# Two 256-column matmuls over one set of weights in place of a 512-column matmul

## The chip, the cores and the metric

The kernel runs on one core of one Trainium2 chip. The metric is the device time of one execution in microseconds (us). The five engines of the core that matter are TensorE (PE in the profile, with its weight loads as PEld), VectorE (DVE), ScalarE (ACT), GpSimd (POOL) and SyncE (SP), whose queue issues nearly all DMAs.

## What is computed

A layer norm of x (2048 tokens by 512) feeds two branches: attention with 32 heads of 16 over a sliding window of 256 tokens, and a SwiGLU block with 1792 hidden columns. The output is x plus the attention branch times silu of the other.

```python
xn = _layernorm(x, axis=-1)
qkv = (xn @ wqkv)                      # 512 -> 3 x 32 heads x 16
scores = einsum("bhqd,bhkd->bhqk", q, k) * 16 ** -0.5
scores = where((i - j >= 0) & (i - j < 256), scores, -1e9)
s = (softmax(scores) @ v) @ wo
g = silu((silu(xn @ w_gate) * (xn @ w_up)) @ w_down)
return x + s * g
```

## The kernel before

All tokens are worked in four chunks of 512. Float32 accuracy is reached with float32r operands: every operand is split into a high and a low part (`xh`, `xl`; `wh`, `wl`; both parts of a hidden block in `hh`), and a product is three matmuls, high by high, high by low and low by high (`PAIRS`).

The array is used in two halves. The contraction is cut into pieces of 64 rows: **half 0** holds rows 0 to 63 and **half 1** rows 64 to 127 of the same weights and inputs, and every matmul is a tile of 64 rows by 128 columns. The two halves run as two streams. Half 0 begins a unit of work, half 1 follows some microseconds later into the same PSUM bank (`LAG`), so at most moments the halves work on different units.

A unit has two items, and an item one PSUM bank of 128 by 512. There are two sorts:

- **Stationary** units (class `Stationary`, lines 509 to 534): the query/key projection (`Proj`, bank `a`) and gate and up (`GateUp`, banks `g` and `u`). The weights stand in the array and 512 tokens of `xh` or `xl` move. An item is 4 pieces of the contraction by 3 pairs, 12 matmuls of 512 columns in each half.
- **Moving** units (class `Moving`, lines 644 to 660): values (`vp`), down (`d`) and output projection (`s`). Here the activations stand in the array and 256 columns of `wh` or `wl` move, two token blocks to a bank.

Between them stand the attention matmuls, which also run on both halves: `b` (row maxima of the scores, 256 or 384 columns, line 963), `mt` (turning the maxima, line 997), `c` (scores for the softmax, line 1114, rows 0 to 48 of a half, with the negated maximum as the 49th row, which the DMA `q<-ms` writes), and `pv` (probabilities by values, line 1151). There are 32 attention units, eight to a chunk.

The order of every engine's instructions is fixed when the program is built, by a planner that keeps a clock of its own for each half. `next_mm` takes one matmul of the half whose clock is behind; `issue` advances that clock by `cols * 0.000444 + 0.004` us, 0.2313 for 512 columns and 0.1177 for 256. The other engines' instructions are put into the program as the planner's clock (`now`) reaches them, by their due times and assumed costs (`do`, `pump`), and a `pv` visit is placed where the two clocks are within 0.12 us of each other and sets both to the same time (`pv_visit`, `advance`). The planner's constants set the order alone; on the chip each instruction waits for its semaphores.

```python
steps = [(k, a, b) for k in range(KC) for a, b in PAIRS]
...
            r = min(able, key=lambda r: clock[r])
            next_mm(r)
```

Of the kernel before, what the change touches and what calls it, by code (L numbers as in the profile page):

```python
# [55 lines left out]
def tile_window_attention_swiglu_gate(  # L56
# [42 lines left out]
    clock = [0.0, 0.0]  # L99
# [124 lines left out]
    xready = {}  # L224
# [104 lines left out]
    xhigh = {}  # L329
# [40 lines left out]
    def half(r):  # L370
        return slice(R * r, R * r + R)
# [92 lines left out]
    def mm(pb, a, b, first, last):  # L464
        return nc.tensor.matmul(pb, a, b, start=first, stop=last, skip_group_check=True)  # L465
# [43 lines left out]
    class Stationary(Unit):  # L509
# [11 lines left out]
        def mms(self, i, r, pb):  # L521
            w = [t.rearrange("p (a k n) -> p a k n", a=2, k=KC) for t in self.wts(r)]
            xs = xn[self.c % 2]
            steps = [(k, a, b) for k in range(KC) for a, b in PAIRS]
            first_unit = self.c == 0 and self.n == 0 and i == 0
            if first_unit:
                steps.sort(key=lambda o: o[2])
            for k, a, b in steps:
                def go(first, last, k=k, a=a, b=b):
                    return mm(pb, w[a][half(r), i, k, :], xs[b][half(r), k, :], first, last)  # L530
                if first_unit:
                    yield 512, go, lambda k=k, b=b: (xready if b else xhigh).get((0, k))
                else:
                    yield 512, go

    class Proj(Stationary):
        def __init__(self, c, pr):
# [755 lines left out]
    front = [0.0]  # L1293
# [6 lines left out]

    def issue(r, cols):
        front[0] = max(front[0], clock[r])
        clock[r] = front[0] + cols * 0.000444 + 0.004

    def next_mm(r):
        if extra[r]:
            cols, go, then = extra[r].pop(0)
            go()
            issue(r, cols)
            if then:  # L1310
                then(clock[r] + 0.25)
            return
# [9 lines left out]
        cols, go = todo[m][:2]  # L1322
        go(r == 0 and m == 0, r == 1 and m == len(todo) - 1)
        issue(r, cols)
        if r == 0 and u.src is not None:
            work[0] += cols * MM / 512
# [62 lines left out]
    while True:  # L1389
        now[0] = max(front[0], min(clock))  # L1390
        while marks and marks[-1][0] <= work[0] / PACE - LEAD:
            _, fn, a = marks.pop()
# [8 lines left out]
        if not any(extra):  # L1401
            s = work[0] / PACE - LEAD
            for st in sorted(streams, key=lambda st: st[-1][0] if st else 1e9):
                if not st:
                    continue
                due, need, fn, a = st[-1]
# [4 lines left out]
                t = need(*a)  # L1411
# [10 lines left out]
        if able:  # L1422
            idle = 0
            r = min(able, key=lambda r: clock[r])
# [7 lines left out]
        if os.environ.get("VIRT"):  # L1432
            u, i = stream[min(pos[0], len(stream) - 1)]
# [40 lines left out]
```

## Time and profile before

| | us |
|---|---|
| median of three runs | 875.1 (871.88 to 876.57) |
| span of the profiled execution, first to last instruction | 873.5 |
| DVE busy | 520.4 (60%) |
| ACT busy | 487.7 (56%) |
| POOL busy | 621.5 (71%) |

The profiled execution's time is given only as its span of 873.5 us, which lies inside the range of the three runs, 1.6 us under their median. DMA moved 139.62 MB at a mean of 160 GB/s. The profile's page has busy time by engine, busy tenths in 40 slices, the chain of work that ended last, and groups of equal instructions (line, engine, operation, tiles written and read, partitions by elements, count; then busy time, mean ns of one and the idle time ahead of them). The timeline lists instructions in order of time: start in us, duration, engine, line, operation, tiles, count; instructions that overlap and are alike share one row with their count. A matmul's duration in these lists (392 to 395 ns for 512 columns) covers its way through the array, and the next matmul of the same half starts well before it is over; how fast a half works is read from the distance between starts.

### The profile page before, as it was taken

Reading aid. Unit: us, or ns where it says so; the run is one execution under the profiler, and the core shown is the slowest. Engines: PE = TensorE matmul, PEld = TensorE weight load, DVE = VectorE, ACT = ScalarE, POOL = GpSimd, SP = SyncE. Lnnn points to the kernel's source line nnn. Section 1 sums busy time; section 2 is a strip of 40 time slices with the busy share of each in tenths; the row PEclk is TensorE's granted clock in tenths of the full one; section 3 lists DMA queues with packets and bytes.
Section 4 is the critical chain, followed back from the end, with each engine's and each line's share of the span. In section 5 each row is a group of like instructions: output and inputs, shape, how many; then the busy total and the mean of one; then the engine's idle time right before and its main releaser. Section 6 shows DMA issues by size and latency. Waiting matters only on the chain.

```text
span 873.5 us, 30184 instructions
## 1 busy us (share of the span) xinstructions
PE 856.1 (98%) x11966; PEld 786.8 (90%) x11966; DVE 520.4 (60%) x1678; ACT 487.7 (56%) x1040; POOL 621.5 (71%) x881
## 2 busy tenths in 40 slices
PE   8999999999999999999999999999999999999997
PEld 7899989897798998989999988899899998998897
DVE  5364476656866565666578675566655775555235
ACT  3355555654665465655576546665656764566531
POOL 5556587766776778767697798677767777868761
PEclk9999999999999999999999999999999999999999
DMA  4775856576786982776687987556666779844442
GB/s 146 183 173 126 228 114 165 114 174 151 164 184 181 256 203 79 155 165 133 149 188 177 230 182 196 116 148 147 166 145 173 174 178 208 181 124 112 107 114 85
DMA packets 69488, 139.62 MB, mean 160 GB/s; under 512 B 14546, under 2 KB 23250, under 8 KB 69348
## 3 DMA queue, kind: packets, MB, share of 16 engines
q1 hardware_dynamic: 69060, 137.18, 65.3%
q8 instruction: 94, 1.54, 0.8%
q10 hardware_dynamic: 288, 0.52, 0.2%
q14 instruction: 46, 0.38, 0.2%
HBM read 107.74 MB, written 29.62 MB: 157 GB/s over the span
## 4 chain that ended last, share of the span: by engine, by line
PE 88%; DVE 4%; POOL 3%; DMA 2%; issue 1%; SPq 0%; ACT 0%; DVEq 0%; POOLq 0%; ACTq 0%
PE u L465 17%; PE d L465 17%; PE g L465 17%; PE a L465 11%; PE pv L1151 8%; PE c L1114 5%; PE s L465 5%; PE vp L465 4%; PE b L963 4%; DMA q<-ms 2%; DVE jk L971 1%; POOL wl L436 1%; DVE xt L287 1%; DMA xt<-x 1%; POOL xt L287 0%
## 5 line engine op out<-in xcount | busy, mean ns | idle before, releaser
L436 POOL TENSOR_TENSOR wl<-wr,wh 128x512 fp32r<-128x512 f32 (+3 forms) x258 | 311.7, 1228 | 92.0 <-ACT wh L433 89.8
L971 DVE CUSTOM_DVE_ANT_0 jk<-b,maskb 128x384 bf16<-128x384 f32 (+2 forms) x512 | 271.1, 529 | 119.3 <-PE b L963 53.1
L1075 ACT ACTIVATE p<-c 128x384 f32<-128x384 f32 (+1 forms) x480 | 209.7, 489 | 135.9 <-PE c L1114 107.3
L465 PE MATMUL d<-wh,hh 64*128 64x256 f32 x1792 | 258.7, 277 | 0.0
L465 PEld LDWEIGHTS d<-wh,hh 64*128 64x128 f32 x1792 | 223.5, 185 | 1.0 <-issue 0.6
L465 PE MATMUL d<-wl,hh 64*128 64x256 f32 x896 | 202.5, 276 | 0.0
L433 ACT ACTIVATE wh<-wr 128x512 fp32r<-128x512 f32 (+3 forms) x258 | 142.2, 593 | 64.4 <-PE u L465 14.1
L1088 POOL TENSOR_SCALAR_AFFINE_SELECT p<-p 128x256 f32<-128x256 f32 x256 | 107.2, 423 | 82.3 <-ACT p L1075 80.7
L465 PE MATMUL u<-xh,wh 64*128 64x512 f32 x448 | 162.1, 395 | 0.0
L465 PE MATMUL u<-xl,wh 64*128 64x512 f32 x448 | 161.3, 395 | 0.0
L465 PE MATMUL u<-xh,wl 64*128 64x512 f32 x448 | 161.3, 394 | 0.0
L465 PE MATMUL g<-xh,wh 64*128 64x512 f32 x448 | 161.2, 395 | 0.0
L465 PE MATMUL g<-xl,wh 64*128 64x512 f32 x448 | 160.6, 394 | 0.0
L465 PE MATMUL g<-xh,wl 64*128 64x512 f32 x448 | 159.4, 394 | 0.0
L465 PEld LDWEIGHTS d<-wl,hh 64*128 64x128 f32 x896 | 148.2, 185 | 0.2
L1114 PE MATMUL c<-q,k 49*128 49x384 f32 (+1 forms) x704 | 117.5, 303 | 3.5 <-DMA q<-ms 2.8
L963 PE MATMUL b<-k,q 48*128 48x384 f32 (+1 forms) x512 | 119.4, 336 | 1.2 <-DVE m L971 0.7
L1092 POOL TENSOR_SCALAR_AFFINE_SELECT p<-p 128x256 f32<-128x256 f32 x224 | 93.3, 417 | 19.0 <-ACT p L1075 18.9
L465 PE MATMUL a<-xh,wh 64*128 64x512 f32 x256 | 96.5, 394 | 0.0
L465 PE MATMUL a<-xh,wl 64*128 64x512 f32 x256 | 96.2, 392 | 0.0
L465 PE MATMUL a<-xl,wh 64*128 64x512 f32 x256 | 96.0, 393 | 0.0
L618 POOL TENSOR_TENSOR hh<-h,hh 128x512 fp32r<-128x512 f32 x56 | 72.9, 1302 | 31.7 <-ACT hh L614 31.0
(110 smaller groups left out, 2087.6 us busy)
## 6 DMA issues: line engine op xcount, KB each, us to landing
wr<-wgu SPq DMA_DIRECT2D x112, 256.0 KB
k<-qkd SPq DMA_DIRECT2D x48, 192.0 KB
wr<-wqk SPq DMA_DIRECT2D x32, 256.0 KB
qkd<-qkh SPq DMA_DIRECT2D x32, 256.0 KB
qkd<-qkl SPq DMA_DIRECT2D x32, 256.0 KB
q<-qkd SPq DMA_DIRECT2D x64, 128.0 KB
wr<-wdn SPq DMA_DIRECT2D x32, 256.0 KB
od<-ev SPq DMA_DIRECT2D x32, 256.0 KB
```

The lines of the kernel that those rows point to most:

```text
L287: (nc.gpsimd if c and i % 2 else nc.vector).tensor_scalar(xt[c, i], xt[c, i], mv[:, i, 0:1], rs[:, i : i + 1], op0=ALU.subtract, op1=ALU.mult)
L433: nc.scalar.activation(hi[0][pr, a:b], raw[pr, a:b], AF.Copy)
L436: nc.gpsimd.tensor_tensor(lo[0][pr, a:b], raw[pr, a:b], f32(hi[0][pr, a:b]), op=ALU.subtract)
L465: return nc.tensor.matmul(pb, a, b, start=first, stop=last, skip_group_check=True)
L618: nc.gpsimd.tensor_tensor(hl[:, 1, :], self.h, f32(hl[:, 0, :]), op=ALU.subtract)
L963: nc.tensor.matmul(pb[:, :w], qs[u % 3][r : r + 48, p, qb * P : (qb + 1) * P], ks[u % 3][r : r + 48, p, lo : lo + w], start=True, stop=True,)
L971: nc.vector.tensor_tensor_reduce(junk[:, :n], pb[:, :n], maskb[:, 3 * P - n :], 1.0, -3.0e38, ALU.add, ALU.max, m[:, col : col + 1],)
L1075: nc.scalar.activation(t[:, h, :], pc[:, a:b], AF.Exp, scale=DH ** -0.5)
L1088: nc.gpsimd.affine_select(s, s, [[0, 2], [1, P]], ALU.is_ge, 0.0, base=0, channel_multiplier=-1)
L1092: nc.gpsimd.affine_select(s, s, [[0, 2], [-1, P]], ALU.is_gt, 0.0, base=0, channel_multiplier=1)
L1114: nc.tensor.matmul(pc[:, at0 : at0 + w], ks[u % 3][r : r + 49, p, k0 : k0 + P], qs[u % 3][r : r + 49, p, qb * P : qb * P + w], start=(i == ...
L1151: nc.tensor.matmul(pbs[r][0][32 * j : 32 * j + 32, q0:q1], vt[half(r), (4 * c + kb) % VT, VW * (4 * g + j) : VW * (4 * g + j) + 32], t[hal ...
```

## The change

`Stationary.mms` yields two matmuls where it yielded one: the first moves tokens 0 to 255 of the chunk into columns 0 to 255 of the bank, the second tokens 256 to 511 into the other half of the bank, both with the same 64 by 128 weights. In `issue` the planner's cost of any 256-column matmul becomes 0.115 us, for the moving units and the attention matmuls of that width too; other widths keep theirs.

```diff
             for k, a, b in steps:
-                def go(first, last, k=k, a=a, b=b):
-                    return mm(pb, w[a][half(r), i, k, :], xs[b][half(r), k, :], first, last)
-                if first_unit:
-                    yield 512, go, lambda k=k, b=b: (xready if b else xhigh).get((0, k))
-                else:
-                    yield 512, go
+                for t in range(2):
+                    tok = slice(256 * t, 256 * t + 256)
+
+                    def go(first, last, k=k, a=a, b=b, tok=tok):
+                        return mm(pb[:, tok], w[a][half(r), i, k, :], xs[b][half(r), k, tok], first, last)
+                    if first_unit:
+                        yield 256, go, lambda k=k, b=b: (xready if b else xhigh).get((0, k))
+                    else:
+                        yield 256, go
...
-        clock[r] = front[0] + cols * 0.000444 + 0.004
+        clock[r] = front[0] + (0.115 if cols == 256 else cols * 0.000444 + 0.004)
```

Two places of TensorE's program show what moves. The names are the bank written, the moving tile and the weights (for `d` the weights are `hh`); the chunk's number is left out of a name, and the last number tells tiles of one name apart.

The first place is in the last chunk, with both halves on up: half 0 on `u_13`, half 1 on `u_12`. Before:

```order
L465 MATMUL u_13_16739<-xh_81,wh_16505 128x512
L465 MATMUL u_12_16665<-xh_81,wh_16505 128x512
L465 MATMUL u_13_16739<-xl_82,wh_16505 128x512
L465 MATMUL u_12_16665<-xl_82,wh_16505 128x512
L465 MATMUL u_13_16739<-xh_81,wl_16506 128x512
L465 MATMUL u_12_16665<-xh_81,wl_16506 128x512
```

And now:

```order
L465 MATMUL u_13_20153<-xh_81,wh_19809 128x256
L465 MATMUL u_12_20031<-xh_81,wh_19809 128x256
L465 MATMUL u_13_20153<-xh_81,wh_19809 128x256
L465 MATMUL u_12_20031<-xl_82,wh_19809 128x256
L465 MATMUL u_13_20153<-xl_82,wh_19809 128x256
L465 MATMUL u_12_20031<-xl_82,wh_19809 128x256
L465 MATMUL u_13_20153<-xl_82,wh_19809 128x256
L465 MATMUL u_12_20031<-xh_81,wl_19810 128x256
```

The halves still alternate one by one, but each step is half as wide and every operand pair of a half comes twice in a row.

The second place is a little later: half 1 is on gate `g_13`, half 0 on the down unit `d_2_0_0`. Before:

```order
L465 MATMUL g_13_16702<-xl_82,wh_16633 128x512
L465 MATMUL d_2_0_0_16776<-wh_16633,hh_7_16011 128x256
L465 MATMUL d_2_0_0_16776<-wh_16633,hh_8_16141 128x256
L465 MATMUL g_13_16702<-xh_81,wl_16634 128x512
L465 MATMUL d_2_0_0_16776<-wl_16634,hh_8_16141 128x256
L465 MATMUL d_2_0_0_16776<-wh_16633,hh_8_16141 128x256
```

And now:

```order
L465 MATMUL g_13_20090<-xh_81,wh_19975 128x256
L465 MATMUL d_2_0_0_20215<-wh_19975,hh_9_19779 128x256
L465 MATMUL g_13_20090<-xh_81,wh_19975 128x256
L465 MATMUL d_2_0_0_20215<-wl_19976,hh_9_19779 128x256
L465 MATMUL g_13_20090<-xl_82,wh_19975 128x256
L465 MATMUL d_2_0_0_20215<-wh_19975,hh_9_19779 128x256
```

Where one `g` stood for two `d`, the halves now take turns with equal steps.

## Prediction

> **What bounds the kernel now.** I read the page first: busy times, granted clock, and the chain that ended last.
>
> ```profile
> PE 856.1 (98%) x11966; PEld 786.8 (90%) x11966; DVE 520.4 (60%) x1678; ACT 487.7 (56%) x1040; POOL 621.5 (71%) x881
> PEclk9999999999999999999999999999999999999999
> PE 88%; DVE 4%; POOL 3%; DMA 2%; issue 1%; SPq 0%; ACT 0%; DVEq 0%; POOLq 0%; ACTq 0%
> ```
>
> TensorE has some matmul in flight for 856.1 of the 873.5 us, at an unthrottled clock, and the chain that set the end runs on it for 88%. DVE, ACT and POOL are busy for 71% at most. So the time is the sum of the steps with which TensorE's two halves take their matmuls, plus the few moments when it waits. What it waits for is in the view of waits, TensorE alone:
>
> ```profile
> PE c L1114 <- DMA q<-ms: 2.8, 3, 1.8
> PE mt L997 <- DVE m L971: 2.6, 3, 1.8
> PE xp L353 <- DVE xt L287: 2.3, 2, 1.5
> ```
>
> All of TensorE's idle time is 873.5 - 856.1 = 17.4 us, a good part of it at the start, and its longest group is 2.8 us. A change of the kernel's time by a per cent must therefore come from the steps. The groups of the page count the matmuls that the change touches:
>
> ```profile
> L465 PE MATMUL u<-xh,wh 64*128 64x512 f32 x448 | 162.1, 395 | 0.0
> ...
> L465 PE MATMUL a<-xh,wh 64*128 64x512 f32 x256 | 96.5, 394 | 0.0
> ```
>
> Up, gate and projection have three such groups each (one for each pair of high and low parts): 3 x 448 + 3 x 448 + 3 x 256 = 3456 matmuls of 512 columns, 1728 in each half. The mean of 395 ns is no step, since matmuls of one half overlap. The step is read in the timeline, where both halves are on up and nothing comes between (start, duration, then the instruction; x2 is one in each half):
>
> ```profile
> 825.05 0.40 PE L465 MATMUL u<-xh,wh 64*128 64x512 f32 x2
> 825.29 0.40 PE L465 MATMUL u<-xl,wh 64*128 64x512 f32 x2
> ...
> 826.92 0.40 PE L465 MATMUL u<-xh,wl 64*128 64x512 f32 x2
> ```
>
> From 825.05 to 826.92 each half takes eight steps: 1.87 / 8 = 0.2338 us. With the 10 ns in which starts are printed this is 233 ns, and 1728 x 0.233 = 403 us, 46% of the span. Any nanosecond on one of these steps is 1.7 us of the kernel's time.
>
> **The change, part by part.** *The step.* The change replaces 1728 steps of 233 ns in each half by 3456 of a 256-column matmul with weights from `wh` or `wl` and moving data from `xh` or `xl`. This operation isn't in the trace of before; call its step p. The sum is 1728 x (2p - 233 ns). Three other 256-column matmuls bound p. The first is down, with both halves on it:
>
> ```profile
> 217.11 0.32 PE L465 MATMUL d<-wh,hh 64*128 64x256 f32 x2
> 217.22 0.27 PE L465 MATMUL d<-wl,hh 64*128 64x256 f32 x1
> 217.27 0.34 PE L465 MATMUL d<-wh,hh 64*128 64x256 f32 x2
> 217.38 0.27 PE L465 MATMUL d<-wl,hh 64*128 64x256 f32 x1
> ...
> 218.13 0.32 PE L465 MATMUL d<-wh,hh 64*128 64x256 f32 x2
> ```
>
> Rows of two and of one alternate, so from 217.11 to 218.13 stand 18 matmuls, nine in each half: 1.02 / 9 = 113.3 ns. The second is values, in one half, while the other is on up:
>
> ```profile
> 439.00 0.39 PE L465 MATMUL u<-xh,wh 64*128 64x512 f32 x1
> 439.00 0.28 PE L465 MATMUL vp<-wh,xl 64*128 64x256 f32 x1
> 439.12 0.27 PE L465 MATMUL vp<-wh,xh 64*128 64x256 f32 x1
> 439.23 0.39 PE L465 MATMUL u<-xl,wh 64*128 64x512 f32 x1
> ...
> 440.16 0.39 PE L465 MATMUL u<-xh,wl 64*128 64x512 f32 x1
> 440.17 0.28 PE L465 MATMUL vp<-wh,xh 64*128 64x256 f32 x1
> ```
>
> `vp` starts at 439.00 and, ten steps on (two to each step of `u`), at 440.17: 117.0 ns. In the same time `u` takes five steps in 1.16 us, 232 ns. The third is the score matmul `c`, 49 rows, two of 256 columns in each half between steps of 512:
>
> ```profile
> 703.23 0.39 PE L465 MATMUL a<-xl,wh 64*128 64x512 f32 x1
> 703.46 0.41 PE L1114 MATMUL c<-q,k 49*128 49x256 f32 x4
> 703.70 0.40 PE L465 MATMUL a<-xh,wl 64*128 64x512 f32 x1
> 703.94 0.40 PE L465 MATMUL a<-xh,wh 64*128 64x512 f32 x1
> ```
>
> The half that works on `a` takes its two `c` from 703.46 to 703.70, so p = 120 ns. The three ends of the sum: with 113.3, 1728 x (226.6 - 233) = -11.1 us; with 117.0, 1728 x (234 - 233) = +1.7 us; with 120, 1728 x (240 - 233) = +12.1 us. **I take 116.5 ns**, half of what 512 columns take now, sum 0. The nearest row is `vp`: it reads the same two sets of buffers as the changed products (`x` and `w`, their roles swapped), while `d` reads the hidden blocks. In the window quoted, `vp` and the 512-column `u` beside it go at the same pace for a column: 117.0 / 256 = 0.457 ns and 232 / 512 = 0.453 ns. So the column, not the instruction, seems to set the step for these buffers, and cutting in two moves nothing.
>
> *The weight loads.* Every matmul of before has a load of its own (11966 and 11966 on the page), also `d`, whose high part stays in the array for two products in a row. So I count on 3456 more loads, over weights that are there already. What hides them is the half's own matmul:
>
> ```profile
> L465 PEld LDWEIGHTS d<-wh,hh 64*128 64x128 f32 x1792 | 223.5, 185 | 1.0 <-issue 0.6
> ```
>
> A load of this shape shows 185 ns, yet down issues one for every step of 113.3 ns in a half, so loads overlap too. Cost beyond p: none. If that cover were gone, p would grow towards the 185 ns of the load.
>
> *The planner's constant and the finer steps.* 0.115 in place of 0.1177 us brings the planned step of the moving units nearer to the traced 113 to 117. It costs no instruction; it shifts where attention matmuls, other engines' work and DMA issues fall in each engine's program. Nothing is moved by more than the drift between two clocks. Bounds from the waits: the three listed above add up to 7.7 us, so -3 to +6 us; I take 0, since the row of waits does not say to which side.
>
> *The `pv` visits.* Each sets both halves to one time, and the half that is ready first waits for the other. The planner allows a visit when its clocks are within 0.12 us; with steps of 233 ns the halves miss each other by up to 117 ns, with 116 ns by up to 58, so on average some 30 ns less. The chain of waits, in order of time, shows one visit thus, and there are 32:
>
> ```profile
> 796.02 2.38 PE pv L1151 x93
> ```
>
> 32 x 0.03 = 1.0 us, an estimate, at the least 0 and at the most twice that. I take -1.0 us.
>
> **The sum:** 0 + 0 + 0 - 1.0 = -1 us on a profiled span of 873.5 us, which gives 872.5. That execution's span is 1.6 us under the median of the runs, and I carry the difference over: 875.1 - 1.0 = **874.1 us**.
>
> **The rivals.** *The step falls to down's 113.3 ns.* For it: down has 256 columns, its own load for each, the same row count, and holds 113.3 whatever the order of its pairs; in the changed program nearly all neighbours have one width, as in that stretch of `d`. Against it: `vp` has all that too and needs 117. Fully, 874.1 - 11.1 = 863.0 us; at 115 ns, 1728 x (230 - 233) = -5.2, 868.9 us.
>
> *A fixed cost for each matmul*, the one that ends slower. Its place is the start of each of the 1728 added steps in a half; `c` shows it, with 120 ns between 512-column steps of 233 to 240. At 120 the kernel takes 874.1 + 12.1 = 886.2 us, at 118.5 it takes 1728 x 4 = 6.9 more, 881.0. It decides from p = 117.8: there the sum passes +4.4 us, half a per cent. Against it: `c` has one row more, other buffers, and weights that change with each piece; `vp` at 117.0 stays below.
> The Trainium skill, "TensorE: Matmul & The Clock Gate", section "Back-to-back issue gap", has the gap as the columns over the clock plus a fixed 2.5 ns for each matmul, so that two of 256 take 2.5 ns longer than one of 512; an estimate from that is 1728 x 2.5 ns = 4.3 us, 878.4 us. The trace differs: twice down's step is less than the 512-column step, twice `vp`'s is about equal, and only `c` goes that way.
>
> *The new order makes new waits.* The DMA `q<-ms` made TensorE wait 3 times in 32 units, 2.8 us, 0.9 us each. Six more such units would be +5.6 us, 879.7. For it: that row is the longest wait, and every transfer's place moves. Against it: TensorE is in no hurry if its steps don't shorten.
>
> *The change does nothing of its kind*, if the built program merged or dropped a load: excluded by the program, where all 3456 pairs stand.
>
> **How the numbers follow.** The same pace for a column (p between 115.5 and 117.8): 0.50, of which with the shift of waits some 0.11 fall below -0.5% and 0.08 above +0.5%. The faster step: 0.27, nearly all of it faster. The fixed cost: 0.15, nearly all slower. New waits alone: 0.08, half slower. This gives faster 0.37, same 0.37, slower 0.26; half a per cent, 4.4 us, is about what a measurement of this kernel can tell from no change. The range must reach into both rivals: down to 865 (p of 114 ns), up to 882 (p of 118.5 with 1 us of waits); left out are about a tenth on each side. The likeliest case alone is 870 to 879.
>
> **What would show it.** In the changed profile's timeline, a stretch with both halves on up: ten steps in 1.13 us say the first rival, 1.17 the forecast, 1.20 the second. The groups must list 6912 matmuls of 256 columns for `a`, `g` and `u`, and as many loads. TensorE's waits should stay near 17 us in all; if they grow by 5 or more, it is the order. The forecast is wrong if the step leaves 115.5 to 117.8, or if one half waits for the other in a way that neither shows as idle.

## The result and the profile after

The changed kernel takes 896.7 us (893.33 to 900.09, four runs) against 873.6 us for the kernel before in the same series: a ratio of 1.0257, 95% interval 1.0229 to 1.0285, so 20 to 25 us slower. The profiled execution has a span of 897.7 us and took 899.62 us. The forecast was 874.1 us, and its range ended at 882.

The page after, the lines that answer to those of before: busy times and the chain that ended last.

```profile
PE 870.8 (97%) x15422; PEld 838.3 (93%) x15422; DVE 527.5 (59%) x1678; ACT 487.5 (54%) x1040; POOL 618.3 (69%) x881
...
PE 77%; DMA 13%; DVE 4%; POOL 2%; SPq 2%; issue 2%; ACT 1%; DVEq 0%; ACTq 0%; POOLq 0%
```

Two things have changed. TensorE has 3456 more matmuls and as many more loads, as the program said, and is busy 14.7 us longer. And its idle time, in which both halves stand still, has grown from 17.4 to 897.7 - 870.8 = 26.9 us. The chain shows the same: it runs through DMAs for 13% of the span, where it was 2%.

The groups of the page (line, engine, operation, tiles; count, busy time and mean ns) count the split products, and the timeline gives their step:

```profile
L465 PE MATMUL u<-xh,wh 64*128 64x256 f32 x896 | 172.9, 280 | 0.0
```

```profile
848.45 0.27 PE L465 MATMUL u<-xh,wh 64*128 64x256 f32 x1
...
851.29 0.27 PE L465 MATMUL g<-xh,wh 64*128 64x256 f32 x1
```

One half begins an item of `u` at 848.45 and the next item, a `g`, at 851.29. An item is now 24 matmuls in each half, so the step is 2.84 / 24 = 118.3 ns, two of them 236.6 where 512 columns took 233.

The waits of TensorE (who waited for whom; total us, times, longest) show where idle time was added:

```profile
PE mt L1000 <- DVE m L974: 6.2, 4, 2.9
PE c L1117 <- DMA q<-ms: 5.4, 6, 1.7
PE d L465 <- DVE ho L462: 2.6, 1, 2.6
```

The turning of the maxima waits 6.2 us for DVE (2.6 before), the scores 5.4 us for the maxima's DMA (2.8 before), and one down unit 2.6 us for DVE's handover copy. These are the waits of one execution: in a second profile of the same kernel, the "change again" below, the turning waits 3.4 us in all, the scores 2.5, and the down unit 2.6 again.

### The profile page after: what moved, and what is told of

It is laid out like the page before. It is cut to its first block, busy times and chain, and to the rows that moved or that the text cites. A ratio compares the mean times of both kernels' runs of the same rounds, so it can differ in the third digit from the quotient of the medians.

```text
span 897.7 us, 37111 instructions
## 1 busy us (share of the span) xinstructions
PE 870.8 (97%) x15422; PEld 838.3 (93%) x15422; DVE 527.5 (59%) x1678; ACT 487.5 (54%) x1040; POOL 618.3 (69%) x881
## 4 chain that ended last, share of the span: by engine, by line
PE 77%; DMA 13%; DVE 4%; POOL 2%; SPq 2%; issue 2%; ACT 1%; DVEq 0%; ACTq 0%; POOLq 0%
PE d L465 16%; PE u L465 14%; PE g L465 13%; PE a L465 8%; PE pv L1154 6%; DMA q<-ms 5%; PE s L465 5%; PE c L1117 5%; PE b L966 4%; PE vp L465 3%; DMA r<-rd 2%; DMA den<-od 2%; SPq L95 2%; DMA k<-qkd 1%; DMA q<-qkd 1%
## 5 line engine op out<-in xcount | busy, mean ns | idle before, releaser
L1078 ACT ACTIVATE p<-c 128x384 f32<-128x384 f32 (+1 forms) x480 | 209.1, 489 | 139.6 <-PE c L1117 117.8
L465 PE MATMUL g<-xh,wh 64*128 64x256 f32 x896 | 173.4, 281 | 0.4 <-issue 0.4
L465 PE MATMUL u<-xh,wl 64*128 64x256 f32 x896 | 172.9, 280 | 0.0
L465 PE MATMUL u<-xh,wh 64*128 64x256 f32 x896 | 172.9, 280 | 0.0
L465 PE MATMUL g<-xl,wh 64*128 64x256 f32 x896 | 172.3, 281 | 0.0
L465 PE MATMUL g<-xh,wl 64*128 64x256 f32 x896 | 172.1, 280 | 0.0
L465 PE MATMUL u<-xl,wh 64*128 64x256 f32 x896 | 170.8, 280 | 0.0
L465 PEld LDWEIGHTS g<-xh,wh 64*128 64x128 f32 x896 | 134.1, 186 | 0.9 <-issue 0.7
L465 PEld LDWEIGHTS g<-xh,wl 64*128 64x128 f32 x896 | 134.4, 187 | 0.4 <-issue 0.2
L465 PEld LDWEIGHTS u<-xh,wh 64*128 64x128 f32 x896 | 133.8, 186 | 0.6 <-issue 0.4
L465 PEld LDWEIGHTS g<-xl,wh 64*128 64x128 f32 x896 | 134.2, 187 | 0.2
```

What stands on the lines that cost most here:

```text
L1078: nc.scalar.activation(t[:, h, :], pc[:, a:b], AF.Exp, scale=DH ** -0.5)
```

## The experiments

The theories. **A:** the step itself is dearer. **B:** the new order of the instructions makes the loss. **C:** the order hurts only because TensorE is slower than the planner's 0.115 us. **D:** each order draws its own waits, spread and by luck. **E:** the order's waits sit at the chunk boundaries, where DVE stands in its queue behind two late DMAs. All ratios are to the kernel before, on the same chip, with their 95% intervals.

### The split in the old order

```diff
-                    return mm(pb, w[a][half(r), i, k, :], xs[b][half(r), k, :], first, last)
+                    for t in range(2):
+                        tok = slice(256 * t, 256 * t + 256)
+                        mm(pb[:, tok], w[a][half(r), i, k, :], xs[b][half(r), k, tok], first and t == 0, last and t == 1)
```

> Both halves of each 512-column product are issued as two 256-column matmuls, but the planner counts them as one step of 512 columns, so all other instructions of every engine stand in the order of before. Theory A (the step itself is dearer: about 118.5 ns in the changed profile against half of 233, 4 to 5 ns for each of 1728 pairs in a half): 8 us over before, about 881 to 883 us. Theory B (the loss is only the new order's waits): within 2 us of before. If the split alone carries the whole loss, about 896.

1.0078 (1.0049 to 1.0106), 880.3 us: 0.0078 x 875 = 6.8 us. The step read from the trace gives (236.6 - 233) x 1728 = 6.2 us. Over some 2600 products that follow each other directly in both profiles, the pair takes 3.9 ns more on the mean than the single matmul of before, which is 6.7 us for 1728. Theory A is right about the step, and the step is under a third of the loss of the first series.

### The planner's constant alone

```diff
-        clock[r] = front[0] + cols * 0.000444 + 0.004
+        clock[r] = front[0] + (0.115 if cols == 256 else cols * 0.000444 + 0.004)
```

> Only the planner's cost of a 256-column matmul becomes 0.115 us; the products stay 512 columns wide. Theory A (the step and the order share the loss): the order moves with little change of the step, so any time over before is waits; some us up to 10. Theory B (the order of the moving units alone makes the waits): most of the 23 us, near 890 or more. If neither the constant nor its order matters: 872 to 876.

1.0033 (1.0012 to 1.0055), 2.9 us. The reordering of the moving units alone costs little.

### Other constants with the split

The changed kernel with the old formula, and with three other constants in place of 0.115:

```diff
-        clock[r] = front[0] + (0.115 if cols == 256 else cols * 0.000444 + 0.004)
+        clock[r] = front[0] + cols * 0.000444 + 0.004
```

> The products are split as in the change, with the planner's old cost (0.1177 us for 256 columns). Theory A: the plan is now close to the traced step of 118.5 ns, so the waits shrink and about 8 us of step remain: 880 to 884. Theory B with the finer steps as the cause of the waits: still 890 or more.

> The change with 0.1185 us in the planner for 256 columns, the traced step. Theory C (the gap between planned and real step makes the waits): 879 to 883, the 6.8 us of the step and no more. Theory D (each constant draws another order, and the waits are luck): anything from 879 to 896, in no order with the constant.

> The change with 0.113 us, further below the real step. Theory C: more waits than with 0.115, over 897. Theory D: anything from 879 to 900.

> The change with 0.1165 us, between the change's 0.115 and the old 0.1177. Theory C: between their times, 886 to 896. Theory D: anything from 879 to 896.

| planned step, us | ratio to before |
|---|---|
| 0.113 | 1.0129 (1.0087 to 1.0171) |
| 0.115 (the change) | 1.0257 (1.0229 to 1.0285) |
| 0.1165 | 1.0241 (1.0186 to 1.0295) |
| 0.1177 (old formula) | 1.0124 (1.0076 to 1.0172) |
| 0.1185 | 1.0115 (1.0068 to 1.0162) |

Theory C wanted more loss at 0.113, further from the real step than 0.115, and the kernel is faster there than the change in its first series; against the repeat of the change (1.0167, below) it is not, beyond the intervals. At 0.1185, the real step, C wanted 879 to 883 us and the kernel takes 885.6. Each of these orders costs something over the 0.8% of the step, from 0.3 to 1.8%, though the three smallest overlap with the interval of the step, and the size doesn't follow the constant: 0.1165 costs more than 0.113 and 0.1177 on either side. No new order was found that beats the old one.

### The change's order with 512-column matmuls

The planner takes its two steps of 256 as in the change, but TensorE gets one 512-column matmul at the second:

```diff
+                held = []
                 for t in range(2):
...
-                        return mm(pb[:, tok], w[a][half(r), i, k, :], xs[b][half(r), k, tok], first, last)
+                        held.append(first)
+                        if t == 1:
+                            return mm(pb, w[a][half(r), i, k, :], xs[b][half(r), k, :], held[0], last)
```

> The planner works as in the change (two steps of 256 columns, 0.115 us each), so DVE, ACT, POOL and SyncE have exactly the instructions of the changed kernel in its order, but TensorE gets one 512-column matmul at the second step of each pair. The split alone cost 6.8 us (its own run), the whole change 23. Theory A (the rest, some 15 us, is waits that the new order makes whatever the step): about 888 to 890. Theory C (the order is harmless by itself and hurts only because TensorE's real step of 118.4 ns is slower than the 115 ns that the planner goes by): 872 to 879.

1.0099 (1.0066 to 1.0132), 8.7 us. So the order does harm by itself, which speaks against C again, but not the 15 us that A had left for it. Its ten runs go from 878.57 us, at a mean granted clock of 0.998, to 889.84 at 0.991, and the profiled execution is that slowest one. TensorE's waits in it show the down unit's wait at the same size as in the changed kernel:

```profile
PE d L465 <- DVE ho L462: 2.6, 1, 2.6
```

### Where the order loses its time

To find the place I compared the start of half 1's last matmul in each unit, a point that all kernels pass, with its start in the profiled execution of before. Each column is one execution; that of "order, 512" is the slowest of its ten, so it shows more than the 8.7 us of the mean. Lateness in us:

| unit | before, us | change | change again | order, 512 | split, old order |
|---|---|---|---|---|---|
| `u` chunk 0, block 11 | 167.5 | 5.2 | 3.8 | 4.0 | 0.5 |
| `d` chunk 0, third quarter | 191.9 | 5.3 | 3.9 | 4.1 | 0.6 |
| `d` chunk 0, last quarter | 218.7 | 9.8 | 9.2 | 8.9 | -0.8 |
| `d` chunk 1, first unit | 324.1 | 10.3 | 8.9 | 7.2 | -0.1 |
| `u` chunk 2, block 4 | 528.5 | 19.0 | 13.9 | 12.7 | 1.6 |
| `g` chunk 3, block 0 | 682.0 | 19.8 | 14.4 | 11.3 | 2.1 |
| `u` chunk 3, block 1 | 704.4 | 24.6 | 15.0 | 11.8 | 2.3 |
| `g` chunk 3, block 12 | 829.7 | 24.3 | 14.6 | 14.5 | 4.2 |

The split in the old order loses its time evenly. The change's order loses it in jumps at the ends of chunks: about 5 us from 192 to 219 in all three kernels that have it. There the chain of waits of the changed kernel runs through one small DMA, and the timeline of DVE (start, duration, instruction; in brackets the idle time ahead and who ended it) shows what stands behind it:

```profile
203.08 9.89 DMA den<-od
```

```profile
212.99 0.35 DVE L862 RECIPROCAL den<-den 128x32 f32<-128x32 f32 x1 [2.95 <-DMA den<-od]
213.26 3.05 DVE L889 TENSOR_TENSOR o<-o,r 128x512 f32<-128x512 f32 x1
...
217.62 0.55 DVE L974 CUSTOM_DVE_ANT_0 jk<-b,maskb 128x384 bf16<-128x384 f32 x1
...
220.23 0.15 DVE L462 COPY ho<-d 80x1 f32<-80x1 f32 x1
```

The sums of the softmax (16 KB) land 9.89 us after they were issued. DVE works in order: the reciprocal waits 2.95 us, the multiplication behind it takes 3.05 us, and the row maxima (`jk`) start at 217.62. Only after the fourth of them comes the handover copy that TensorE's down unit waits for until 220.43. The DVE of before at the same place:

```profile
207.52 0.35 DVE L859 RECIPROCAL den<-den 128x32 f32<-128x32 f32 x1
...
208.43 2.34 DVE L886 TENSOR_TENSOR o<-o,r 128x512 f32<-128x512 f32 x1
210.69 0.55 DVE L971 CUSTOM_DVE_ANT_0 jk<-b,maskb 128x384 bf16<-128x384 f32 x1
```

Two `jk` and the reciprocal are done by 207.87, the reciprocal finds its data there, and the other two `jk` start at 210.69. TensorE waits here too, but 1.8 us.

TensorE's waits show only part of the loss. In the changed kernel one half alone works on `d` for some 4 us before both stand:

```profile
216.06 0.39 PE L465 MATMUL d<-wh,hh 64*128 64x256 f32 x2
216.29 0.27 PE L465 MATMUL d<-wl,hh 64*128 64x256 f32 x1
216.40 0.39 PE L465 MATMUL d<-wh,hh 64*128 64x256 f32 x2
```

Three steps take 0.34 us, 113 ns each: that is the pace of a single half, where both together start about six in that time. By the order of the program, half 1 stands from 213.8 to 220.43, 6.6 us, until the handover copy; the 2.6 us among the waits are only the end of this, when half 0 stands as well. In before, half 1 stands 2.0 us at this place. Added up over an execution (gaps of over 0.3 us between the matmuls of a half, beyond their step, without the `pv` visits and the first 20 us), a half stands 13 to 14 us in before, 29 in the changed kernel, 19 to 20 in its repeat, 25 in "order, 512", and 14 to 15 in the split in the old order.

The clock comes on top. Around some of these waits the granted clock falls to a half for 3.4 or 6.8 us. The view of busy times by stretch shows it from 220.8, 493.9 and 719.2 us on in the changed kernel, 3.4 us each, from 217.3 (6.8 us) and 490.4 in the repeat, from 216.9 (6.8 us), 449.0 and 725.5 in "order, 512", from 212.5 (3.4 us) in before, and not at all in the split in the old order, apart from the last few us of every kernel. The page shows the longest of them, here that of "order, 512", and in the timeline of the changed kernel a step of 256 columns takes about 215 ns there:

```profile
PEclk9999999998999999999999999999999999999999
```

```profile
719.50 0.41 PE L465 MATMUL u<-xh,wh 64*128 64x256 f32 x1
...
719.93 0.41 PE L465 MATMUL u<-xl,wh 64*128 64x256 f32 x1
```

A stretch of 3.4 us at half the clock does up to 1.7 us less work, by estimate: up to 5.1 us in the changed profile and 1.7 in that of before. In the runs the mean granted clock is 0.9925 for the change, 0.9948 for its repeat, 0.9945 for "order, 512", and 0.9974 to 0.9977 for before in the series that list it. What brings the clock down was not tested; a wait of 1.8 us for `q<-ms` in before has no such stretch after it.

### The change and its order without the two DMA waits

In both kernels, changed and "order, 512", DVE is freed of what `den<-od` and `r<-rd` bring, with every instruction in its place; the kernel leaves out the division by the softmax sum:

```diff
-            nc.vector.reciprocal(box[0], box[0])
+            box.append(sb(f"rcp{c}_{k}", [P, 32], F32, "rcp", 2))
+            nc.vector.reciprocal(box[1], warm[:, :32])
...
-            move(rd[c, hd].rearrange("h (a n) -> (h a) n", n=32), box[0])
+            move(rd[c, hd].rearrange("h (a n) -> (h a) n", n=32), box[1])
...
-            nc.vector.tensor_tensor(box[0], box[0], box[1], op=ALU.mult)
+            nc.vector.tensor_tensor(box[0], box[0], box[0], op=ALU.mult)
```

> The changed kernel with the same instructions in the same order, but the reciprocal on DVE no longer reads what the DMA den<-od brings (it takes a tile of ones), and the multiplication of the attention output no longer reads what r<-rd brings (it squares o); the DMAs themselves still run. So the division by the softmax sum is left out. Theory E (at the chunk boundaries DVE stands in its queue behind these two late DMAs, the row maxima behind it are late, and TensorE waits for them; in the changed profile DVE waits 10.5 us for them, before 2.1): a good part of the 15 us beyond the step goes, 883 to 890. Theory D (the waits are spread over many places, and others take over): 892 to 898, as the change.

> The changed kernel once more, on the same chip and beside the same runs of before as the two others: 895 to 899 as at first, so that the difference to the run without the two DMAs is free of differences between chips.

> The run with the change's order but 512-column matmuls, and DVE freed of the same two DMAs as in the run without them (the division by the softmax sum is left out again). With the two DMAs it took 8.7 us over before. Theory E (in the new order DVE's waits at the chunk boundaries are most of what the order costs): 2 to 5 us over before, 877 to 880, and the progress curve without its step near 192 to 219 us. Theory D (the order's cost is spread): 883 to 886.

With the split: 1.0107 (1.0062 to 1.0152) without the two waits, and 1.0167 (1.0096 to 1.0239) for the change itself beside it. The difference of 0.6%, 5 us, is as theory E wants it, but the intervals overlap, and by itself it settles nothing. In its profile another jump follows in place of the first, 3.6 us between 241 and 255 on the scale of the table, where TensorE waits 1.6 us for `q<-ms` and the clock falls to a half from 254.9 on. The changed kernel came out faster than in its first series, and not as expected.

With 512 columns: 1.0035 (1.0013 to 1.0056) without the waits, 1.0099 with them, and these intervals lie apart: 0.64%, 5.6 of the 8.7 us. But the two numbers are of different series on different chips, and the changed kernel came out 0.9% apart in two series, so the size isn't firm. Part of it is the clock: the mean granted clock is 0.9975 without the waits, as for before, and 0.9945 with them, by estimate 0.0030 x 885 = 2.7 us. The places agree. In the first kernel the lateness goes from 4.4 to 5.0 us between 191.9 and 218.7, in the second from 2.5 to 2.7, where it had jumped by 4.5 and 4.8. The DVE of the changed kernel without the two waits, in the same queue order:

```profile
209.04 0.34 DVE L863 RECIPROCAL rcp<-warm 128x32 f32<-128x32 f32 x1
209.37 0.92 DVE L890 TENSOR_TENSOR o<-o 128x512 f32<-128x512 f32 x1
...
213.34 0.55 DVE L975 CUSTOM_DVE_ANT_0 jk<-b,maskb 128x384 bf16<-128x384 f32 x1
```

and TensorE's longest wait for DVE's maxima, over the whole execution:

```profile
PE mt L1001 <- DVE m L975: 0.9, 2, 0.6
```

The maxima come at 213.34, 4.3 us sooner, the turning waits 0.9 us in all, where it waits 3.4 in the change beside it and 6.2 in the first profile, and the down unit's wait for DVE is gone. Not all of this need be the DMA: the multiplication, which now reads `o` alone, takes 0.92 us in place of 3.05. Theory E holds for this place. That the two waits carry most of the order's cost, 5.6 of 8.7 us, is likely but not shown. DVE's total wait for the two DMAs is no measure of the loss: it is 2.1 us in before and 10.5 in the change, but also 8.8 in the split in the old order, which loses little beyond its step, and 16.7 with the constant 0.1185. What matters is what stands behind the wait, and for the rest of the cost, some 3 us, D is left.

### Four matmuls of 128 columns

What makes the step of 118 ns? If each added matmul has a fixed price, four quarters cost three times as much as two halves.

```diff
-                    for t in range(2):
-                        tok = slice(256 * t, 256 * t + 256)
+                    for t in range(4):
+                        tok = slice(128 * t, 128 * t + 128)
```

> As the first run of the split, each product in the order of before, but as four matmuls of 128 columns in place of one of 512. Theory A1 (a fixed cost of some 4 ns for each added matmul: 6.9 us for 1728 in a half, so three times that for 5184): 895 to 897. Theory A2 (with half the columns the weight load of 128 columns is no longer covered and sets the step): well over 910; if a 128-column step were as long as a 256-column one, 118 ns, it would be some 410 us more.

1.6037 (1.5968 to 1.6106), or 1405 us; the profiled execution, with a lower granted clock (0.918 in place of 0.937), has a span of 1430.7. A fixed price alone would have given 895. The timeline, one half on `u`, the other on `g`:

```profile
1384.87 0.27 PE L465 MATMUL u<-xh,wh 64*128 64x128 f32 x1
...
1384.98 0.27 PE L465 MATMUL u<-xh,wh 64*128 64x128 f32 x1
...
1386.10 0.27 PE L465 MATMUL u<-xh,wl 64*128 64x128 f32 x1
```

Between the first and the last row the half on `u` takes 11 steps in 1.23 us: 111.8 ns each, where a quarter of 233 would be 58. A quarter of the columns takes nearly as long as half of them (118 ns). So in these runs there is a floor of some 112 ns under each matmul with its load. What a fixed price adds above the floor, in the step of 118 ns, the quarters can't tell: by 3.6 ns for each matmul they would step in some 61 ns, and the floor hides that. In this stretch four quarters take 447 ns for 233, and (447 - 233) x 1728 = 370 us of the 1430.7 - 873.5 = 557 that this span is longer. The other 187 us I haven't separated. A good part of them is the clock, by estimate up to (1 - 0.918) x 1430.7 = 117 us. The page shows it as low as five tenths early on:

```profile
PEclk7555559999988998999999999999999999999999
```

The Trainium skill, "TensorE: Matmul & The Clock Gate", section "LDWEIGHTS (loading the stationary operand)", has the load as its columns over 1.2 GHz, whatever its rows: 107 ns for 128 columns, within 5 ns of the floor. That names the load as the likely cause of the floor; no run here took the load away and left the matmul, so it isn't shown. Between 25 and 185 us, where the granted clock is 0.50, the same step takes 213 ns, so the floor goes with the clock.

### The inputs moved by 32 bytes

In the trace of before, 256-column steps depend on where the weights come from (113.3 ns from the hidden tiles, 117 from the `x` tiles), and the two differ in their place modulo 64 bytes.

```diff
+    pers.tile([P, 8], F32, name="pad0")
     xn = [[pers.tile([P, KC, TC], F32R, name=f"x{'hl'[s]}{i}") for s in range(2)] for i in range(2)]
+    pers.tile([P, 8], F32, name="pad1")
```

> The kernel before, with the normalized inputs (the xh and xl tiles) 32 bytes further on in each partition and everything behind them 64 bytes further; same instructions in the same order. In the trace of before, 256-column steps with weights from the hidden tiles (32 bytes off a multiple of 64) take 113.3 ns and those with weights from the x tiles (on a multiple) 117. If the place sets this, vp falls to about 113 to 114 ns and the 512-column step perhaps to 227 ns: up to 11 us less, 863. If it does not, within 1 us of before.

0.9991 (0.9972 to 1.0010): no difference. The place isn't the cause; what makes down's step shorter stays open.

## Why the prediction was wrong

The main lines of the forecast's reading hold: TensorE sets the end, one nanosecond on the touched steps is 1.7 us, and the program carries all the added matmuls and loads. The two terms that were put at zero failed, both towards slower. Taken alone, the split costs 6.8 us and the order 8.7 us, together 15.5 us; the change cost 23 us in its first series and 1.67%, 14.6 us, in the repeat. The clock was not quite unthrottled, as the prediction read from tenths: in the profile of before it stands at a half for 3.4 us from 212.5 on.

**The step, p = 116.5 ns: mis-sized.** The trace shows 118.3, inside the bounds of 113.3 to 120, but beyond the 117.8 from which the second rival was to decide. The term is 1728 x (236.6 - 233) = +6.2 us in place of 0, and the split in the old order takes 6.8. The reason given, that the column and not the instruction sets the step, because `vp` and the 512-column `u` beside it go at one pace for a column, was a reading of 4 ns in rows printed to 10 ns. Which row was nearest hung on the buffers, and that they decide is not shown. What I should have kept is that two of the three rows for 256 columns, `vp` and `c`, stood above half of 233.

**The rival of a fixed cost** had the sign right, and its point at 118.5 ns, 6.9 us, is the size measured. As the whole mechanism it falls: a fixed price per matmul would make quarters cost three times the halves, about 20 us, and they cost over 500. For the halves it isn't excluded, since the floor hides any such price in the quarters. The 2.5 ns for each matmul that the Trainium skill gives ("TensorE: Matmul & The Clock Gate", "Back-to-back issue gap") make 4.3 us by estimate, against 6.8 measured: the right direction, and about two thirds of it.

**The weight loads, "cost beyond p: none": the reason was too weak.** I looked at the 185 ns that a load shows, saw down issue one for every 113.3 ns, and concluded that loads overlap. They do, but the steps with a 128-column load of their own that were read here end at about 112 ns. A 512-column step has 121 ns to spare above that floor, one of 256 columns 6. Down's 113.3, which I took as the sign of a cheaper step, stands right at it. Halving goes to the edge; the next halving falls off. Why up takes 118 and not 112 there, the floor alone doesn't say, so for the halves it isn't shown that the loads cost anything.

**The planner's constant and the finer steps: the term that failed most.** I took 0, with +6 us at the most, and wrote that nothing is moved by more than the drift between two clocks. The change's order with 512-column matmuls costs 8.7 us. The bound was taken from TensorE's own waits of before, and those say nothing of a new order: a new wait arises on DVE, behind `den<-od` and `r<-rd`, two DMAs for which DVE waited 2.1 us before and waits 10.5 us in the change. With them taken out of DVE's way the jump near 219 us goes, and the cost falls from 8.7 to 3.1 us, measured in another series. The constant alone, with the old widths, costs 2.9 us; the finer steps together with it cost the 8.7.

**The rival of new waits** was the right kind and the wrong place. It named `q<-ms`, which grew from 2.8 to 5.4 us in the first profile and was 2.5 in the repeat; more came through DVE, where the turning went from 2.6 to 6.2 us (3.4 in the repeat) and the down unit's 2.6 us were new in both. My argument against it, that TensorE is in no hurry if its steps don't shorten, looked at TensorE's speed. What matters is what stands ahead in DVE's queue. TensorE's idle time grew by 9.5 us in the first profile, where I had set 5 as the sign that it is the order, but only from 17.4 to 18.8 us in the repeat. The better sign was the last one of the prediction, one half waiting in a way that neither shows as idle. In the first profile a half stands about 15 us more than before; with 6.2 us of step and up to 3.4 us of clock that makes some 25 us, by estimate, for the 24.2 between the two profiles. In the repeat 6, 6.2 and up to 3.4 us make some 16 for 14.6.

**The `pv` visits, -1.0 us:** no run tests them. The split in the old order leaves every visit where it stood, and in the others the order changes with it. A gain of 1 us is neither shown nor excluded.

**What stays open.** The first series of the change is some 7 us above the sum of its parts, the repeat is not. In the first profile the lateness grows by 4.8 us between 682.0 and 704.4, in the repeat's by 0.6, with the same program. What differs there is one instruction of DVE, ahead of the maxima:

```profile
712.29 4.25 DVE L752 SCALAR_TENSOR_TENSOR gp<-dt,t 128x512 f32<-128x512 f32 x1
```

It takes 4.25 us, in the repeat 1.58, and 0.69 in the median of the sixteen of its sort. The turning then waits 2.9 us (0.2 in the repeat), and the clock stands at a half from 719.2 on, as it does not there in the repeat. Why one instruction takes so long is open: GpSimd is busy beside it from 712.0 to 716.0, but no run shows that it holds DVE up. Open too: why down steps in 113.3 ns and up in 118.3, what brings the clock down, and where the last 3 us of the order's cost lie.

## What to carry to other kernels

Before a moving tile is cut, compare its time with the shortest step at which matmuls with a load of their own follow each other in the same trace: here 233 ns had 121 to spare over 112, and 118 has 6. Where a scheduler decides the order, make the change once with the old order held fixed and once as the order alone; here that gave two parts that were each measurable, 6.8 and 8.7 us. Repeat the change itself in a second series, since here that moved its cost from 23 to 14.6 us. Where an engine works in two halves, count the standing of each half, not only the idle time of both. And price a new order by the in-order queues: ask which instruction would now stand behind a late DMA on an engine that looks idle, since the waits of the old order don't show it.

## What the runs showed of the hardware that was not expected

- With a load for each, matmuls of 128 columns in one half follow each other in 111.8 ns, those of 256 in 118.3, those of 512 in 233. Halves are nearly free, quarters cost 60% of the kernel's time, of which up to 88 us of some 530 may be a lower clock (0.937 in the two shorter runs, by estimate). At a granted clock of 0.50 the step of 128 columns is 213 ns.
- Around some waits of TensorE of 1.6 to 3.1 us the granted clock falls to a half for 3.4 or 6.8 us, and a 256-column step goes from 118 to about 215 ns. The ten runs of "order, 512" go from 878.57 us at a mean clock of 0.998 to 889.84 at 0.991.
- A planned step of 0.113 us gave 1.0129, 0.115 gave 1.0257 and 0.1177 gave 1.0124: the cost of an order follows no line in its constant.
- A 16 KB transfer took 9.89 us to land in a stretch in which the DMA engines moved 156 GB/s, the mean of the whole execution. With 512 columns, the kernel whose DVE waits neither for it nor for the other transfer (`r<-rd`) was 5.6 us faster, in another series, though DVE is only 59% busy.
- The same program gave 1.0257 (1.0229 to 1.0285) in one series and 1.0167 (1.0096 to 1.0239) in another: intervals that just overlap, with midpoints 8 us apart.
